# Four 256 KB transfers for each group of w_in, two groups issued one period ahead, and x's last rows sent by GpSimd's queue

## The chip, the cores and the metric

The kernel runs on one core of one Trainium2 chip. The metric is the device time of one execution in microseconds. Engine names are those of the profile: PE (TensorE), PEld (its weight loads), DVE (VectorE), ACT (ScalarE), POOL (GpSimd), SP (SyncE), which here only issues transfers; a q behind a name is the engine's queue.

## The reference, cut to what matters

Two blocks follow each other. The first is an mLSTM cell over 768 steps with 4 batches, 8 heads and a head dimension of 40; the second a feed-forward block on 3072 tokens of width 320, with 2048 inner columns.

```python
m_new = max(f + m, i);  f_stab = exp(f + m - m_new);  i_stab = exp(i - m_new)   # each step t
C = f_stab * C + i_stab * outer(v, k);   n = f_stab * n + i_stab * k
y = sigmoid(o) * (C @ q) / max(abs(n . q), 1)
...
x = y as (tokens, heads * 40)
h = x @ w_in;   g = h * cos(h);   out = g @ w_out
```

w_in (320 x 2048) and w_out (2048 x 320) come in 64-bit floats: each number is two 32-bit words, and the kernel makes 32-bit floats of them on the chip.

## The kernel before, in words

**Work and its order.** The 768 steps are six chunks of 128 (c = 0 to 5). A cell n is one chunk of one batch, n = 4c + b. The first four cells, chunk 0, are done by `first_cells` (a start-up of some 43 us). After that `both_parts(c, b)` does two things at once: the feed-forward block of chunk c, and the cell of batch b of chunk c + 1. One call of it is called a period here; it has two slots, i = 0 and i = 1, each with two of the sixteen column blocks of w_in (`f2 = 2b + i`). In a slot PE multiplies x with w_in (`Up`, L645 and L651), ACT and DVE make h cos h of it (`near` L659, `rest` L662, `sin` L667, `gate` L671), and PE multiplies an earlier slot's result with w_out (`down` L683, or in later chunks `products`, L761). The two PSUM banks of a slot are free for the next slot once both gates have run. Everything is emitted in an order written out by hand: each engine carries out its instructions in the order of the text.

**The cell.** In slot 0 come scores (L485), decay (L394, L408), values (L511 to L520) and `normalize_turned` (L529 to L540), which writes x into `xT`. `fade` (L586, four instructions on POOL) multiplies the running state by its decay; `state` (L628, four on DVE, in slot 1) adds the cell's share. Chunks 0 to 3 of the feed-forward block carry cells with fade and state; the cells of the last chunk have neither.

**x's last rows.** 256 of the 320 rows of x are in `xT`; the 64 last ones have to stand in `xL` twice, at partitions 0 and 64. For cells from the fifth on two transfers of 32 KB copy them there (L610), in `seam_out`, at the start of slot 1, from ACT's queue.

**Weights.** Chunk 0's periods also bring in the weights. w_in comes in four groups f of 512 columns. Of each, `weights_in` makes three pieces: two of 128 partitions (one for each half of 256 rows), each by four transfers of 128 KB (L139, 32 rows of 4 KB), and one for the last 64 rows by four of 64 KB (L180). w_out comes in eight pieces p by one transfer of 640 KB each (L186). Raw words land in buffers named `bits`: four buffers of pool `pb` for w_in (and, later, for the tiles `D` of `sums`), three of `pc` for w_out. A piece is converted by `take_apart` (ACT, L154 and L156), `bound` (DVE, L160 and L161) and `put_together` (DVE L167, then POOL L168). Group 1 is converted in `first_cells`, group 2 in period b = 0, group 3 in b = 1, group 4 in b = 2. Groups 3 and 4 are issued at the end of periods b = 0 and b = 1.

**Queues.** Nearly all transfers are issued by SP's queue in the text's order, so an issue that waits for a buffer holds back all behind it. In this framework the transfers of SP's and ACT's queues share eight completion semaphores in turn: a transfer is issued only when the eighth one before it has landed. Those of POOL's queue have eight of their own.

Of the kernel before, what the change touches and what calls it, by code (L numbers as in the profile page):

```python
# [11 lines left out]
FP = mybir.dt.float32  # L12
I32 = mybir.dt.int32
# [16 lines left out]
def kernel(  # L30
# [32 lines left out]

    NK = DM // 128
# [9 lines left out]
    pe = ctx.enter_context(tc.tile_pool(name="pe", bufs=3))  # L74
    po_s = ctx.enter_context(tc.tile_pool(name="po_s", bufs=4))
    p1 = ctx.enter_context(tc.tile_pool(name="p1", bufs=1))
    pb = ctx.enter_context(tc.tile_pool(name="pb", bufs=4))
    pc = ctx.enter_context(tc.tile_pool(name="pc", bufs=3))
    dram = ctx.enter_context(tc.tile_pool(name="dram", bufs=1, space=bass.MemoryType.DRAM))
    ps_a = ctx.enter_context(tc.tile_pool(name="ps_a", bufs=2, space=bass.MemoryType.PSUM))  # L80
# [50 lines left out]


    WP, WQ = 512, 2 * DM
    w_in_bits, w_out_bits = (w.bitcast(I32).rearrange("r (n two) -> r n two", two=2) for w in (moe_w_in, moe_w_out))

    def bits_in(n, src, pool, width):
        bits = pool.tile([128, width, 2], I32, name="bits", tag="bits")
        for rows, piece in src:
            nc.sync.dma_start(out=bits[rows, 0:n], in_=piece)  # L139
        return bits  # L140

    def to_float32(*made):
        for dst, bits in made:
# [27 lines left out]
    w_in_last = moe_w_in.bitcast(I32).rearrange("(h d) (a e n) -> e a h d n", d=D, e=2, n=2 * 128)[:, :, :, 32:D]  # L171

    def weights_in(f):
        for i in range(NK):
            src = [(slice(32 * a, 32 * a + 32), w_in_bits[D * (NK * a + i):D * (NK * a + i) + 32, ts(f, WP)]) for a in range(HP)]
            yield w_in_sb[:, i, ts(f, WP)], bits_in(WP, src, pb, WP)
        bits = pb.tile([128, WP, 2], I32, name="bits", tag="bits")
        for e in range(2):
            for a in range(2):
                nc.sync.dma_start(out=bits[64 * e:64 * e + 64, ts(a, 128)].rearrange("r n two -> r (n two)"), in_=w_in_last[e, 2 * f + a])  # L180
        yield w_in_l[:, ts(f, 2)].rearrange("p a n -> p (a n)"), bits


    def weights_out(p):
# [403 lines left out]
    def seam(n):  # L588
# [9 lines left out]
        if n < N - B:  # L598
# [4 lines left out]
                    nc.tensor.matmul(pu[64 * j:64 * j + D, p], kws[n][:, h, 0:D], vs(n)[:, h], start=True, stop=True)  # L603
            pus[n] = pu

    def seam_out(n):
        c, b = divmod(n, B)
        if n >= B:
            for e in range(2):
                nc.scalar.dma_start(out=xL[c][64 * e:64 * e + 64, b], in_=ys[n][0:128:2])  # L610
            return
        if b == 0:
            new_x(c)
        nc.scalar.copy(out=xT[c][:, NK * b:NK * b + NK], in_=pxs[n][:, 0:NK])
# [96 lines left out]

    def sums(c, k):

        if k % 4 == 0:
            Ds[c, k // 4] = pb.tile([128, 4, 2, C], FP, name="D", tag="bits")
        D1, D4 = (Ds[c, k // 4][:, k % 4, i] for i in range(2))
        S = Ss[c, k] = p2.tile([128, 4, C], FP, name="S", tag="S")
        G0, G1 = (gs[c, 2 * k + e].rearrange("q (p e t) -> q p e t", p=2, e=2) for e in range(2))
        tt = nc.vector.tensor_tensor
        tt(out=S[:, 2], in0=G0[:, 0, 1], in1=G1[:, 0, 1], op=OP.add)  # L720
        tt(out=S[:, 0], in0=S[:, 2], in1=G0[:, 0, 0], op=OP.subtract)
        tt(out=S[:, 3], in0=G1[:, 0, 0], in1=S[:, 0], op=OP.subtract)
        tt(out=G0[:, 0, 1], in0=G0[:, 0, 0], in1=G0[:, 0, 1], op=OP.subtract)
        tt = nc.gpsimd.tensor_tensor
        tt(out=D1, in0=G0[:, 1, 1], in1=G1[:, 1, 1], op=OP.add)  # L725
        tt(out=S[:, 1], in0=D1, in1=G0[:, 1, 0], op=OP.subtract)
        tt(out=D4, in0=G1[:, 1, 0], in1=S[:, 1], op=OP.subtract)
        tt(out=G0[:, 1, 1], in0=G0[:, 1, 0], in1=G0[:, 1, 1], op=OP.subtract)
# [2 lines left out]

    def products(c, k):

        S, D1, D4 = Ss[c, k], *(Ds[c, k // 4][:, k % 4, i] for i in range(2))
# [12 lines left out]
        banks = [id(t) for t, *_ in made]  # L747
        for j, (t, i, lhs, rhs) in enumerate(made):

            yield t[:, i], lhs, rhs, k == 0 and id(t) not in banks[:j], k == LAST and id(t) not in banks[j + 1:]  # L750

    def late_products(c):
        L = late[c] = ps_o.tile([128, 2, HALF], FP, name="late", tag="o")
        for k in range(NF // 2):
            for i, rhs in ((0, wv[:, k, 0, 1]), (1, wv[:, k, 1, 1])):
                yield L[:, i], Ds[c, k // 4][:, k % 4, i], rhs, k == 0 and i == 0, k == LAST and i == 1

    def run(made, n):
        for _ in range(n):
# [75 lines left out]
    def first_cells():  # L835
# [108 lines left out]
        turn_blocks(B)  # L944
        state(3)
        load_E(B + 2)
        decay(B)
        sigmoid(1)
        weigh_k(B)
# [16 lines left out]
    def both_parts(c, b):  # L966

        n = (c + 1) * B + b
        cell = n < N
        for i in range(2):  # L970
# [14 lines left out]
            if i == 0:  # L985
                if cell:
                    weigh(n)
                    if n + 1 < N:
                        decay_exponents(n + 1)
                    if n == B:  # L990
                        clear_low()
                for e in range(2):
                    up.sin(e)
                    up.gate(e)
                if c > 0:
                    sums(c, f2)
                if b == 0 and c == 1:
                    sigmoid(c + 1)

                if c == 0:  # L1000
                    next_out(*[pieces.pop(0) for _ in range(min(b, len(pieces), 1))])
                if cell and n + 1 < N:
                    decay(n + 1)
            else:
                if cell:
                    seam_out(n)
                if cell:
                    state(n)
                for e in range(2):
                    up.sin(e)  # L1010
                    up.gate(e)
                if c > 0:
                    sums(c, f2)
                if n == B + 1:
                    low_dimensions(n + 1)
                if c == 0:
                    next_out(*pieces)
                    pieces.clear()
                if cell and n + 1 < N:
                    if c > 0:  # L1020
                        weigh_k(n + 1)
                    odd_values(n + 1)
# [7 lines left out]
            if cell and i == 0:  # L1030
                turn_gate(n)
                values(n)
                seam(n)
                normalize_turned(n)
                fade(n)
                if c == 1 and b < 3:
                    weight_sums(b + 1)
                if n % 2 == 1 and n > B + 1 and n + 3 < N:
                    load_two(n + 3, "qk")
                if n > B + 1 and n + 3 < N:  # L1040
                    load_E(n + 3)
                if b == B - 2 and c + 2 < NC:
                    load_o(c + 2)
                if c == 0 and pieces:
                    to_float32(pieces.pop(0))
                sin_next()
            if f2 == 0 and c > 1:
                for p in range(2):
                    combine(c - 1, p)
            if i == 1:  # L1050
                if c == 0 and b + 2 < B:
                    pieces.extend(weights_in(b + 2))
                    load_two((n + 3) // 2 * 2)
# [9 lines left out]
    pieces, outs = [], []  # L1063
    with tc.manual_schedule():
        first_cells()
        for c in range(NC):
# [38 lines left out]
```

## Time and profile before

| | us |
|---|---|
| median of 3 runs (lowest, highest) | 542.03 (541.94, 544.99) |
| span of the profiled execution | 541.8 |
| PE busy | 518.0 (96%) |
| DVE busy | 420.1 (78%) |
| ACT busy | 285.1 (53%) |
| POOL busy | 227.0 (42%) |
| moved by DMA | 57.81 MB, mean 107 GB/s |

The page gives one execution, taken by the hardware profiler. Its own time is the span from the first to the last instruction; no other time of this execution is shown, and the median of the runs lies 0.2 us above it. Busy shares are means over stretches with different limits: start-up to about 43 us, the four periods of chunk 0 to about 143 us, and the rest.

### The profile page before, as it was taken

To read this page: it belongs to the slowest core of one execution; us is meant where nothing else is said; L and a number is where in the kernel's file an instruction comes from. 1 tells how busy PE (TensorE), PEld (TensorE's weight loads), DVE (VectorE), ACT (ScalarE), POOL (GpSimd) and SP (SyncE) were. 2 spreads that over 40 slices of the span, in tenths; PEclk is the share of its full clock that TensorE was granted. 3 is DMA by queue.
4 is the path that set the end of the run, shared out by engine and by line. 5 is a ranking of instruction groups with operands and counts; after the bars stand their busy time and mean duration, and the time that the engine had idled before them with its cause. 6 is when DMAs were issued, how large, how long until landed. Compare 5 with 4: busy or idle time off the path is not lost.

```text
span 541.8 us, 10496 instructions
## 1 busy us (share of the span) xinstructions
PE 518.0 (96%) x3844; PEld 349.5 (65%) x3844; DVE 420.1 (78%) x907; ACT 285.1 (53%) x546; POOL 227.0 (42%) x369
## 2 busy tenths in 40 slices
PE   7997889879999999999999999999999999999996
PEld 4874545545566666766767757757757767576755
DVE  5864978689688897898887898888898878673636
ACT  2876938496395355836436836526836522222221
POOL 7535354446376665434443533543422421221211
PEclk9968889999999999999999999999999999999999
DMA  9999759489677737519439329249320000010001
GB/s 137 209 199 222 220 151 214 131 164 246 137 124 178 104 94 168 63 68 208 46 95 189 41 82 198 44 107 178 38 93 7 2 5 6 10 41 1 0 1 48
DMA packets 99940, 57.81 MB, mean 107 GB/s; under 512 B 62305, under 2 KB 92609, under 8 KB 99889
## 3 DMA queue, kind: packets, MB, share of 16 engines
q1 hardware_dynamic: 96496, 55.64, 48.3%
q10 hardware_dynamic: 3248, 1.33, 1.2%
q8 instruction: 30, 0.49, 0.4%
q14 instruction: 22, 0.17, 0.1%
q0 software_dynamic: 144, 0.18, 0.1%
HBM read 51.71 MB, written 4.11 MB: 103 GB/s over the span
## 4 chain that ended last, share of the span: by engine, by line
PE 75%; DVE 9%; DMA 7%; POOL 2%; SPq 2%; ACT 2%; issue 2%; DVEq 0%; POOLq 0%; ACTq 0%
PE pup L651 27%; PE acc L761 23%; PE pup L645 8%; PE po L683 3%; PE ps L485 3%; PE late L761 3%; DMA E<-M_d 2%; PE vt L520 2%; DMA bits<-in_moe_w_in_dram 2%; PE vt L511 2%; DMA xL<-xT 1%; PE pu L603 1%; DVE g L671 1%; DMA vs<-in_v_dram 1%; SPq L330 1%
## 5 line engine op out<-in xcount | busy, mean ns | idle before, releaser
L651 PE MATMUL pup<-xT,w_in_sb 128*128 128x512 f32 x384 | 178.4, 607 | 5.2 <-DVE g L671 2.5
L659 ACT ACTIVATE n<-pup 128x512 int32<-128x512 f32 x96 | 53.6, 593 | 194.1 <-PE pup L645 142.6
L651 PEld LDWEIGHTS pup<-xT,w_in_sb 128*128 128x128 f32 x384 | 70.3, 192 | 93.0 <-issue 88.1
L662 DVE SCALAR_TENSOR_TENSOR n<-pup,n 128x512 f32<-128x512 f32 x96 | 62.9, 687 | 80.1 <-ACT n L659 78.7
L725 POOL TENSOR_TENSOR D<-g 128x128 f32<-128x128 f32 x40 | 19.9, 497 | 218.2 <-DVE g L671 218.2
L667 ACT ACTIVATE n<-n 128x512 f32<-128x512 f32 x96 | 57.7, 628 | 23.1 <-DVE n L662 15.4
L671 DVE SCALAR_TENSOR_TENSOR g<-pup,n 128x512 f32<-128x512 f32 x96 | 61.6, 683 | 3.9 <-ACT n L667 3.3
L761 PE MATMUL acc<-w_out_sb,g 128*128 128x160 f32 x320 | 58.6, 304 | 0.0
L761 PE MATMUL acc<-T,g 128*128 128x160 f32 x320 | 58.0, 301 | 0.1
L645 PE MATMUL pup<-xL,w_in_l 64*128 64x512 f32 x192 | 54.3, 642 | 1.3 <-POOL w_in_l L168 1.3
L761 PEld LDWEIGHTS acc<-w_out_sb,g 128*128 128x128 f32 x320 | 47.7, 190 | 5.6 <-issue 4.2
L761 PEld LDWEIGHTS acc<-T,g 128*128 128x128 f32 x320 | 48.1, 190 | 3.7 <-issue 3.0
L408 ACT ACTIVATE E<-E,tab 128x128 f32<-128x128 f32 x160 | 49.0, 389 | 0.3
L683 PE MATMUL po<-w_out_sb,g 128*128 128x320 f32 x128 | 36.4, 437 | 1.5 <-POOL w_out_sb L168 1.5
L761 PE MATMUL acc<-T,S 128*128 128x160 f32 x160 | 35.0, 300 | 0.0
L485 PEld LDWEIGHTS ps<-t,t 40*128 40x128 f32 x384 | 24.6, 188 | 12.5 <-DVE t L458 6.6
L683 PEld LDWEIGHTS po<-w_out_sb,g 128*128 128x128 f32 x128 | 23.8, 190 | 13.4 <-POOL w_out_sb L168 3.1
L645 PEld LDWEIGHTS pup<-xL,w_in_l 64*128 64x128 f32 x192 | 14.6, 186 | 25.1 <-issue 19.8
L491 DVE TENSOR_TENSOR E<-ps,E 128x512 f32<-128x512 f32 x48 | 30.6, 679 | 0.0
L761 PE MATMUL acc<-w_out_sb,S 128*128 128x160 f32 x160 | 28.8, 299 | 0.0
L958 ACT ACT_TABLE_LOAD x22 | 28.2, 1283 | 0.4
L761 PEld LDWEIGHTS acc<-T,S 128*128 128x128 f32 x160 | 26.2, 190 | 3.0 <-issue 3.0
(175 smaller groups left out, 878.8 us busy)
## 6 DMA issues: line engine op xcount, KB each, us to landing
E<-M_d SPq DMA_DIRECT2D x22, 512.0 KB
qr<-in_q_dram SPq DMA_DIRECT2D x36, 160.0 KB
kr<-in_k_dram SPq DMA_DIRECT2D x36, 160.0 KB
G<-G_d SPq DMA_DIRECT2D x20, 256.0 KB
bits<-in_moe_w_out_dram SPq DMA_DIRECT2D x8, 640.0 KB
bits<-in_moe_w_in_dram SPq DMA_DIRECT2D x32, 128.0 KB
out_dram<-o_sb SPq DMA_DIRECT2D x24, 160.0 KB
ks<-in_k_dram SPq DMA_DIRECT2D x10, 320.0 KB
```

The source lines that it names most:

```text
L408: nc.scalar.activation(out=Es[n][:, h], in_=Es[n][:, h], func=AF.Exp, scale=-1.0, bias=tab[:, c, 0, g:g + 1])
L485: nc.tensor.matmul(ps[j][:, p], kT[r, p], qT[r, p], start=True, stop=True)
L491: nc.vector.tensor_tensor(out=w, in0=pss[n][j], in1=w, op=OP.mult)
L645: nc.tensor.matmul(pu, w_in_l[r, f2], xL[c][r].rearrange("p b t -> p (b t)"), start=ahead, stop=not ahead)
L651: nc.tensor.matmul(pu.rearrange("p (b t) -> p b t", b=B), w_in_sb[:, i, ts(2 * f2 + e, 128)], xT[c][:, i:NK * B:NK], start=(i == 0 and not ...
L659: nc.scalar.activation(out=self.n[e], in_=self.pu[e], func=AF.Copy, bias=0.25)
L662: nc.vector.scalar_tensor_tensor(out=self.n[e].bitcast(FP), in0=self.pu[e], scalar=0.25, in1=self.n[e], op0=OP.add, op1=OP.subtract)
L667: nc.scalar.activation(out=r, in_=r, func=AF.Sin, scale=TWO_PI_DOWN)
L671: nc.vector.scalar_tensor_tensor(out=g, in0=self.pu[e], scalar=TWO_PI, in1=self.n[e].bitcast(FP), op0=OP.mult, op1=OP.mult)
L683: nc.tensor.matmul(po[c][b], gs[c, f][:, ts(b, C)], w_out_sb[:, f], start=(f == 0), stop=(f == NF - 1))
L761: nc.tensor.matmul(a, lhs, rhs, start=start, stop=stop)
L958: nc.scalar.activation(out=spot, in_=spot, func=AF.Sin)
```

## The change

Three things change.

- Each group of w_in is one buffer `bits` of twice the size (pool `pb` has two instead of four), filled by four transfers of 256 KB, each with 32 rows of both halves. The last 64 rows go to a tile `low` of pool `p2`, with the same four transfers of 64 KB. The tile `D` of `sums` is one for all eight k instead of two for four each.
- The transfers of group 3 are issued at the end of `first_cells`, those of group 4 in period b = 0: each one period earlier than before. The conversions keep their places.
- The two transfers of x's last rows go from ACT's queue at the start of slot 1 to POOL's queue in slot 0, right behind `normalize_turned` and ahead of `fade` (`low_out`).

```diff
-    pb = ctx.enter_context(tc.tile_pool(name="pb", bufs=4))
+    pb = ctx.enter_context(tc.tile_pool(name="pb", bufs=2))
...
+    w_in_heads = moe_w_in.bitcast(I32).rearrange("(a e d) m -> a d e m", e=NK, d=D)
...
     def weights_in(f):
-        for i in range(NK):
-            src = [(slice(32 * a, 32 * a + 32), w_in_bits[D * (NK * a + i):D * (NK * a + i) + 32, ts(f, WP)]) for a in range(HP)]
-            yield w_in_sb[:, i, ts(f, WP)], bits_in(WP, src, pb, WP)
-        bits = pb.tile([128, WP, 2], I32, name="bits", tag="bits")
+        bits = pb.tile([128, NK, WP, 2], I32, name="bits", tag="bits")
+        for a in range(HP):
+            nc.sync.dma_start(out=bits[32 * a:32 * a + 32].rearrange("r i n two -> r i (n two)"),
+                              in_=w_in_heads[a, 0:32, :, ts(f, 2 * WP)])
+        low = p2.tile([128, 2 * 128, 2], I32, name="low", tag="S")
         for e in range(2):
             for a in range(2):
-                nc.sync.dma_start(out=bits[64 * e:64 * e + 64, ts(a, 128)]..., in_=w_in_last[e, 2 * f + a])
+                nc.sync.dma_start(out=low[64 * e:64 * e + 64, ts(a, 128)]..., in_=w_in_last[e, 2 * f + a])
...
+    def low_out(n):
+        c, b = divmod(n, B)
+        for e in range(2):
+            nc.gpsimd.dma_start(out=xL[c][64 * e:64 * e + 64, b], in_=ys[n][0:128:2])
+
     def seam_out(n):
         c, b = divmod(n, B)
-        if n >= B:
-            for e in range(2):
-                nc.scalar.dma_start(out=xL[c][64 * e:64 * e + 64, b], in_=ys[n][0:128:2])
-            return
...
-        if k % 4 == 0:
-            Ds[c, k // 4] = pb.tile([128, 4, 2, C], FP, name="D", tag="bits")
+        if k == 0:
+            Ds[c] = pb.tile([128, NF // 2, 2, C], FP, name="D", tag="bits")
...
         load_E(B + 2)
+        ahead.append(weights_in(2))
...
-                if cell:
-                    seam_out(n)
...
                 normalize_turned(n)
+                low_out(n)
                 fade(n)
...
             if i == 1:
+                if c == 0 and ahead:
+                    pieces.extend(ahead.pop(0))
+                if c == 0 and b == 0:
+                    ahead.append(weights_in(3))
                 if c == 0 and b + 2 < B:
-                    pieces.extend(weights_in(b + 2))
                     load_two((n + 3) // 2 * 2)
                     load_E(n + 3)
```

More of the change, by code (lines that the diff above doesn't have):

```diff
@@ L133 @@
     WP, WQ = 512, 2 * DM
[L134 to L140, printed above, removed]
+    w_out_bits = moe_w_out.bitcast(I32).rearrange("r (n two) -> r n two", two=2)
+    w_in_heads = moe_w_in.bitcast(I32).rearrange("(a e d) m -> a d e m", e=NK, d=D)
     def to_float32(*made):
@@ L173, in weights_in @@
     def weights_in(f):
-        for i in range(NK):
-            src = [(slice(32 * a, 32 * a + 32), w_in_bits[D * (NK * a + i):D * (NK * a + i) + 32, ts(f, WP)]) for a in range(HP)]
-            yield w_in_sb[:, i, ts(f, WP)], bits_in(WP, src, pb, WP)
-        bits = pb.tile([128, WP, 2], I32, name="bits", tag="bits")
+        bits = pb.tile([128, NK, WP, 2], I32, name="bits", tag="bits")
[3 more added lines that the diff above has]
+        low = p2.tile([128, 2 * 128, 2], I32, name="low", tag="S")
         for e in range(2):
             for a in range(2):
-                nc.sync.dma_start(out=bits[64 * e:64 * e + 64, ts(a, 128)].rearrange("r n two -> r (n two)"), in_=w_in_last[e, 2 * f + a])
-        yield w_in_l[:, ts(f, 2)].rearrange("p a n -> p (a n)"), bits
+                nc.sync.dma_start(out=low[64 * e:64 * e + 64, ts(a, 128)].rearrange("r n two -> r (n two)"), in_=w_in_last[e, 2 * f + a])
+        return [(w_in_sb[:, i, ts(f, WP)], bits[:, i]) for i in range(NK)] + [(w_in_l[:, ts(f, 2)].rearrange("p a n -> p (a n)"), low)]
     def weights_out(p):
@@ L712, in sums @@
     def sums(c, k):
-        if k % 4 == 0:
-            Ds[c, k // 4] = pb.tile([128, 4, 2, C], FP, name="D", tag="bits")
-        D1, D4 = (Ds[c, k // 4][:, k % 4, i] for i in range(2))
+        if k == 0:
+            Ds[c] = pb.tile([128, NF // 2, 2, C], FP, name="D", tag="bits")
+        D1, D4 = (Ds[c][:, k, i] for i in range(2))
         S = Ss[c, k] = p2.tile([128, 4, C], FP, name="S", tag="S")
@@ L732, in products @@
     def products(c, k):
-        S, D1, D4 = Ss[c, k], *(Ds[c, k // 4][:, k % 4, i] for i in range(2))
+        S, D1, D4 = Ss[c, k], *(Ds[c][:, k, i] for i in range(2))
         G0, G1 = (gs[c, 2 * k + e].rearrange("q (p e t) -> q p e t", p=2, e=2) for e in range(2))
@@ L755, in late_products @@
             for i, rhs in ((0, wv[:, k, 0, 1]), (1, wv[:, k, 1, 1])):
-                yield L[:, i], Ds[c, k // 4][:, k % 4, i], rhs, k == 0 and i == 0, k == LAST and i == 1
+                yield L[:, i], Ds[c][:, k, i], rhs, k == 0 and i == 0, k == LAST and i == 1
     def run(made, n):
@@ L1061, in both_parts @@
                     weight_sums(0)
-    pieces, outs = [], []
+    pieces, outs, ahead = [], [], []
     with tc.manual_schedule():
```

## The prediction

> **What bounds the kernel now.** I began with the busy time of each engine by stretch. The stretches below are the end of the start-up, the four periods of part c = 0 (b = 0 to 3) and all that follows; the columns are the length, the busy time of PE, PEld, DVE, ACT and POOL (instructions in brackets), the granted clock, the DMA share and GB/s.
>
> ```profile
> 27.00:43.00 16.00, 14.49 (x132) 11.50 (x129) 10.60 (x25) 10.53 (x27) 4.77 (x5) 0.66 0.95 191
> 43.00:68.30 25.30, 21.42 (x137) 12.08 (x138) 17.95 (x39) 22.25 (x48) 11.64 (x14) 0.88 0.88 229
> 68.30:95.30 27.00, 23.33 (x146) 12.62 (x144) 21.96 (x46) 16.20 (x31) 13.84 (x13) 0.94 0.81 185
> 95.30:121.50 26.20, 21.86 (x145) 12.23 (x145) 20.31 (x44) 17.25 (x34) 12.37 (x13) 1.00 0.65 144
> 121.50:143.30 21.80, 21.57 (x145) 12.64 (x146) 18.53 (x40) 13.70 (x25) 8.86 (x10) 1.00 0.73 177
> 143.30:541.80 398.50, 392.32 (x2960) 271.26 (x2958) 312.79 (x681) 190.18 (x362) 157.71 (x276) 1.00 0.38 80
> ```
>
> From 143.3 us on PE is busy 392.3 of 398.5 us: nothing that feeds it earlier can gain much there. The period of b = 3, with no w_in left to convert, takes 21.8 us; those of b = 1 and b = 2 have the same matmuls and take 27.0 and 26.2. So the timeline of PE in these two comes next: start, duration, instruction, and in square brackets the idle time before it and who ended it.
>
> ```profile
> 72.63 3.49 PE L651 MATMUL pup<-xT,w_in_sb 128*128 128x512 f32 x4 [2.48 <-POOL w_in_sb L168]
> ...
> 95.26 3.67 PE L651 MATMUL pup<-xT,w_in_sb 128*128 128x512 f32 x8 [1.19 <-DVE g L671]
> 100.21 1.13 PE L645 MATMUL pup<-xL,w_in_l 64*128 64x512 f32 x4 [1.28 <-POOL w_in_l L168]
> ...
> 115.55 4.57 PE L683 MATMUL po<-w_out_sb,g 128*128 128x320 f32 x16 [1.47 <-POOL w_out_sb L168]
> 121.47 3.67 PE L651 MATMUL pup<-xT,w_in_sb 128*128 128x512 f32 x8 [1.34 <-DVE g L671]
> ```
>
> Converted weights and the gate come late. The timelines of ACT and DVE say why:
>
> ```profile
> 82.37 0.68 ACT L154 ACTIVATE w_in_sb<-bits 128x512 f32<-128x512 f32 x1 [2.37 <-DMA bits<-in_moe_w_in_dram]
> ...
> 108.50 0.68 ACT L154 ACTIVATE w_in_sb<-bits 128x512 f32<-128x512 f32 x1 [4.49 <-DMA bits<-in_moe_w_in_dram]
> ```
>
> ```profile
> 83.08 0.43 DVE L160 TENSOR_SCALAR w_in_sb<-w_in_sb 128x512 f32<-128x512 f32 x1 [1.37 <-ACT w_in_sb L154]
> 84.41 0.49 DVE L160 TENSOR_SCALAR w_out_sb<-w_out_sb 128x640 f32<-128x640 f32 x1 [0.43 <-ACT w_out_sb L154]
> ...
> 109.22 0.43 DVE L160 TENSOR_SCALAR w_in_sb<-w_in_sb 128x512 f32<-128x512 f32 x1 [3.48 <-ACT w_in_sb L154]
> 110.47 0.49 DVE L160 TENSOR_SCALAR w_out_sb<-w_out_sb 128x640 f32<-128x640 f32 x1 [0.36 <-ACT w_out_sb L154]
> ```
>
> ACT waits for the raw w_in of the group (third and fourth group), and DVE behind it for 1.80 and 3.84 us. The transfers were issued late because SP's queue stood at a w_out issue whose buffer was not yet free:
>
> ```profile
> 61.28 14.49 SPq L186 DMA_DIRECT2D bits<-in_moe_w_out_dram  x2
> 75.83 4.38 SPq L139 DMA_DIRECT2D bits<-in_moe_w_in_dram  x8
> ...
> 90.51 11.57 SPq L186 DMA_DIRECT2D bits<-in_moe_w_out_dram  x2
> 102.13 4.20 SPq L139 DMA_DIRECT2D bits<-in_moe_w_in_dram  x8
> ```
>
> **A: groups 3 and 4 one period ahead.** The order of the changed program puts group 3 right ahead of the issue at 61.28, and group 4 where group 3 stands now, at 75.83. Every engine's compute keeps its order. Group 3 is 1.25 MB and joins transfers that end by 70 us; behind them the DMA engines are free (third row):
>
> ```profile
> 28.00:30.00 2.00, 2.00 (x19) 1.95 (x20) 1.54 (x3) 1.96 (x5) 1.09 (x2) 1.00 0.70 168
> 30.00:32.00 2.00, 1.69 (x26) 1.45 (x24) 1.90 (x7) 1.98 (x6) 1.01 (x2) 1.00 0.56 161
> ...
> 70.00:72.00 2.00, 0.15 (x1) 0.00 (x0) 1.99 (x4) 0.00 (x0) 0.76 (x1) 1.00 0.05 16
> ```
>
> At the 185 to 229 GB/s of the periods' rows it takes 5.5 to 6.8 us, so it is in place by about 76 us, and ACT needs it at 80.00 (82.37 - 2.37). Group 4 lands some 20 us ahead of its use at 104. The w_out piece pushed back by eight issues is converted only from 96 us on. Both DMA waits of ACT go, and with them DVE's.
>
> What PE gets of it: in b = 1 DVE and POOL run 1.80 us earlier up to the gate at 94.42, so PE's 1.19 goes whole. The 1.28 in front of L645 shrinks: its weights come 1.80 earlier, PE 1.19, so 1.28 - 0.61 = 0.67 stays. In b = 2 the chain is 1.80 + 3.84 = 5.64 earlier and PE 1.80: there are 3.84 us to cover the waits of 1.47 and 1.34 (2.81), so both go. A = 1.19 + 0.61 + 1.47 + 1.34 = 4.61. The 2.48 at 72.63 stays: it belongs to group 2, whose data was there, and is DVE's order of work. Bounds: 0 if the data comes no earlier, 5.28 if the 0.67 goes too.
>
> **B: four transfers of 256 KB.** By the semaphores of the built program a transfer of SP or ACT waits for the eighth one before it. With 128 KB and 64 KB pieces eight in flight are few bytes, and at 28 to 32 us the DMA engines were busy only 0.70 and 0.56 of the time, which leaves 0.60 + 0.88 = 1.48 us unused, in a stretch (27 to 43 us, first row of all) where their share is 0.95. Four issues fewer, twice as large, let SP run ahead there. What follows in the queue ends in x's gates o, for which ACT waits:
>
> ```profile
> 50.23 1.28 ACT L321 ACT_TABLE_LOAD   x1 [2.51 <-DMA o<-in_o_gate_dram]
> ```
>
> In the rest of this period ACT is busy 22.25 of 25.30 us and sets its pace, so what o gains, PE gains. Bounds 0 and 1.48 (of the 2.51); I take 1.2, near the upper one because that share is so high: what is issued earlier there also lands earlier. Against it: the first half of a group now waits for all four transfers, not for the first four of eight. That is at most half the group later, but the group as a whole is not, and ACT comes to it after both halves have landed.
>
> **C: x's last rows by GpSimd.** Two issues per cell leave ACT's queue and stand on POOL between the weights' or sums' work and the fade of the state; they wait for xT (L540), and behind them wait the four fade instructions, for these DVE's state update (L628), for it the gate (L671), and for its first half PE's next L651. Twenty cells have the pair. What POOL pays for one pair, here the two of G, and when such transfers land:
>
> ```profile
> 21.01 1.10 POOL L264 DMA_DIRECT2D G_d<-kr  x2
> ```
>
> ```profile
> M_d<-kr POOLq DMA_DIRECT2D x1, 80.0 KB, 4.3
> G_d<-kr POOLq DMA_DIRECT2D x2, 40.0 KB, 2.8
> ```
>
> Call a pair's price x; the row says 1.10 us (80 runs of 512 B each; xL has 64). The tightest part is c = 1:
>
> ```profile
> 174.56 1.38 POOL L586 TENSOR_TENSOR st<-st,tab 40x128 f32<-40x128 f32 x4
> ...
> 177.22 1.01 DVE L540 TENSOR_TENSOR xT<-yt,db 128x384 f32<-128x384 f32 x1
> ...
> 180.39 0.86 DVE L628 TENSOR_TENSOR st<-st,pu 40x128 f32<-40x128 f32 x4
> 181.28 1.29 DVE L671 SCALAR_TENSOR_TENSOR g<-pup,n 128x512 f32<-128x512 f32 x2
> ...
> 182.21 3.60 PE L651 MATMUL pup<-xT,w_in_sb 128*128 128x512 f32 x8
> ```
>
> The fade ends at 178.23 + x + 1.38; the last of the four updates begins at 180.39 + 0.65 = 181.04, and PE has 0.28 more (first gate done at 181.93, PE at 182.21). So PE waits from x = 1.71 on. In c = 2 and 3 there are 5.03 us from L540's end to PE against 3.98 here, so from x = 2.76:
>
> ```profile
> 255.06 0.56 DVE L540 TENSOR_TENSOR xT<-yt,db 128x384 f32<-128x384 f32 x1
> ...
> 260.65 3.60 PE L651 MATMUL pup<-xT,w_in_sb 128*128 128x512 f32 x8
> ```
>
> In c = 0, b = 1, the same sum with these rows:
>
> ```profile
> 89.40 1.98 POOL L586 TENSOR_TENSOR st<-st,tab 40x128 f32<-40x128 f32 x4
> 90.12 0.56 DVE L540 TENSOR_TENSOR xT<-yt,db 128x384 f32<-128x384 f32 x1
> 93.53 0.87 DVE L628 TENSOR_TENSOR st<-st,pu 40x128 f32<-40x128 f32 x4
> 94.42 1.29 DVE L671 SCALAR_TENSOR_TENSOR g<-pup,n 128x512 f32<-128x512 f32 x2
> ```
>
> 94.18 - 90.68 - 1.98 = 1.52, and once A has run PE comes 0.80 after the first gate: from x = 2.32. With x = 1.10 nothing waits: the price is 0, hidden by the 0.6 to 1.2 us that are left. The landing (2.8 to 4.3 us) is far ahead of the next use, two matmul slots later. I add 0.2 for extra contention of POOL and DVE; lower bound 0, since ACT's later queue is off the path. ACT gains the time of two issues, which PE does not see.
>
> The Trainium skill (page "SBUF — State Buffer", section "SBUF: two separate sides") speaks against C: while VectorE is in a 2-port mode GpSimd cannot write the descriptors of its own transfers, and one that takes about 620 ns alone takes about 3100 ns beside a VectorE copy. No row here shows it; by its figure x would be about 6.2 in c = 0, where L160 follows L540 at once, which is an estimate of +11.6 us over three cells and 548 us in all.
>
> **Sum.** The profiled execution's span is 541.8; the median of the runs, 542.03, lies 0.2 above it. 541.8 - 4.61 - 1.2 + 0.2 = 536.2, and 536.4 as a median.
>
> **Rivals.** (1) DVE is the bound once the waits are gone. For it: it is busy 21.96 and 20.31 us in the two periods, and beside POOL its instructions can stretch, as the row of L167 shows (minimum, median, maximum in ns):
>
> ```profile
> L167 DVE SCALAR_TENSOR_TENSOR w_out_sb<-bits,w_out_sb x8: 816/822/1900, 58.3 to 143.4; 128x640 int32<-128x640 int32 x8
> ```
>
> One such stretch (1.08) in each period and B at 0: 541.8 - 4.61 + 2.16 + 0.2 + 0.2 = 539.8. Against it: b = 2 has 1.03 us in hand. (2) Slower: POOL is held until its transfer lands. Then x is 2.8 to 4.3; at 3.55, three cells of c = 0 lose 1.23, four of c = 1 lose 1.84, eight of c = 2 and 3 lose 0.79: 17.4 us, or 553.6. It decides from about x = 2.8, where the losses (6.1) eat the gain. Against it: the pair of G took 1.10 with landings of 2.8. (3) The early issue brings nothing, as the DMA engines are full then: 542. Against it: the share of 0.05 at 70 us. (4) More: o gains all 2.51, and the four L651 at 72.63, 0.87 us each against 0.46 in the row at 95.26, run at full clock (1.66 less): 541.8 - 4.61 - 2.51 - 1.66 + 0.2 = 533.2. Against it: the 2.48 ahead of them stays.
>
> **How the numbers follow.** Forecast 59%, with its own range 535.0 to 537.8; (1) 17%, (4) 12%, (2) 8%, (3) 4%. One per cent of 542.03 is 5.4 us, so 536.6 is the limit, about what a measurement of this kernel can tell from no change; two thirds of the forecast's chance lie below it, as I left out small waits of PE that A also shortens. Faster: 39 + 12 = 51%. Within: 20 + 17 + 4 = 41%. Slower: 8%. The range, 533.6 to 540.2, leaves out (2), (3) and the far side of (4).
>
> **What would show it.** Right: no DMA wait of ACT at L154 in b = 1 and b = 2, periods of about 22 us, o's wait near 1.3 us, a pair of xL issues at 1.1 us on POOL, no wait of L628 for the fade. Wrong: PE waiting for L671 behind L586 in c = 1 (C's step), or b = 1 and b = 2 as long as before with the data there (A's step).

## The result, and the profile after

| | before | after |
|---|---|---|
| median of the runs, us | 541.99 | 539.40 (537.49 to 540.78) |
| span of the profiled execution, us | 541.8 | 538.5 |
| ratio of the times, first comparison | 1 | 0.993, 95% interval 0.9907 to 0.9953 |
| ratio, second comparison (`changed_again` below) | 1 | 0.991, 95% interval 0.9882 to 0.9939 |

The change brings 0.7 to 0.9% by the two ratios (the two medians of the first row alone give 0.5%): inside the range of the prediction, 3 us short of its 536.4, and on the side "within 1%" that it held for the less likely. Single executions of the kernel before lie at 541.6 to 545.7 us, so the ratios, and not two medians, are what to compare. The profiled execution of `ab_low_by_act` below ran at a mean clock of 0.649 (757 us) and a second one took 1824 us, so both are left out of its ratio and its steps are read from `ab_again`, the same kernel.

The busy time by stretch, after, columns as in the prediction (its last column pairs are granted clock, DMA share, GB/s):

```profile
27.00:43.00 16.00, 15.90 (x168) 14.06 (x167) 8.82 (x23) 13.38 (x33) 6.56 (x6) 0.82 1.08 189
43.00:68.30 25.30, 24.55 (x163) 12.96 (x163) 19.59 (x45) 21.51 (x47) 12.65 (x16) 0.83 1.02 250
68.30:95.30 27.00, 23.19 (x146) 13.14 (x146) 23.46 (x49) 18.47 (x37) 14.96 (x16) 0.94 0.88 173
95.30:121.50 26.20, 25.35 (x157) 13.98 (x157) 24.19 (x51) 17.73 (x33) 16.11 (x18) 1.00 0.97 201
121.50:143.30 21.80, 21.80 (x152) 13.14 (x149) 16.52 (x34) 12.84 (x24) 10.74 (x14) 1.00 1.08 200
143.30:538.50 395.20, 388.80 (x2947) 269.46 (x2944) 311.75 (x677) 191.28 (x362) 171.18 (x305) 1.00 0.35 75
```

The stretches are those of the prediction, so after the change the same stretch holds more of the work: that of b = 2 has 157 of PE's instructions instead of 145, and PE is busy for 25.35 instead of 21.86 of its 26.20 us. PE's timeline shows which waits are left (line numbers are 3 or 4 lower than before: L648 was L651, L642 was L645):

```profile
57.06 0.42 PE L507 MATMUL vt<-E,vs 128*32 128x128 f32 x8 [0.43 <-issue]
69.31 1.10 PE L648 MATMUL pup<-xT,w_in_sb 128*128 128x512 f32 x2 [0.93 <-DVE g L668]
74.14 2.56 PE L648 MATMUL pup<-xT,w_in_sb 128*128 128x512 f32 x4 [2.88 <-POOL w_in_sb L163]
99.42 1.13 PE L642 MATMUL pup<-xL,w_in_l 64*128 64x512 f32 x4 [0.64 <-POOL w_in_l L163]
...
138.42 3.60 PE L648 MATMUL pup<-xT,w_in_sb 128*128 128x512 f32 x8
```

The waits of 1.19, 1.47 and 1.34 us are gone, the 1.28 is 0.64, the 2.48 has stayed (2.88), and one of 0.93 is new. ACT's conversions of groups 3 and 4 begin with no wait, since the transfers were issued 18 us (58.25 against 75.83) and 25 us (77.36 against 102.13) earlier:

```profile
81.29 0.66 ACT L149 ACTIVATE w_in_sb<-bits 128x512 f32<-128x512 f32 x1
...
103.13 0.67 ACT L149 ACTIVATE w_in_sb<-bits 128x512 f32<-128x512 f32 x1
```

```profile
58.25 2.23 SPq L171 DMA_DIRECT2D bits<-in_moe_w_in_dram  x4
...
77.36 1.87 SPq L171 DMA_DIRECT2D bits<-in_moe_w_in_dram  x4
```

For all that follows, three marks on PE's timeline divide an execution: the first values of the period b = 0 (57.06 above), the first `Up` of c = 1 (138.42 above), and the end. Before, the first two stand here:

```profile
55.63 0.46 PE L511 MATMUL vt<-E,vs 128*32 128x128 f32 x8 [3.88 <-issue]
...
143.09 3.60 PE L651 MATMUL pup<-xT,w_in_sb 128*128 128x512 f32 x8
```

So the start-up went from 55.63 to 57.06 (+1.43), chunk 0 from 87.46 to 81.36 (-6.10), and what follows from 541.8 - 143.09 = 398.7 to 538.5 - 138.42 = 400.1 (+1.4): the gain is in chunk 0, and two losses take nearly half of it back. By the first values of each period, b = 0 takes 27.09 us (27.01 before), b = 1 22.21 (24.54), b = 2 21.02 (24.87), and from there to the second mark it is 11.04 in both. So the gain of chunk 0 is in b = 1 (2.33) and b = 2 (3.85), at full clock in both kernels. These two periods, before and then after (columns as above):

```profile
82.64:107.18 24.54, 21.82 (x145) 12.24 (x144) 20.17 (x43) 17.02 (x33) 12.66 (x13) 1.00 0.77 167
107.18:132.05 24.87, 21.82 (x145) 12.24 (x144) 21.48 (x46) 18.60 (x34) 12.14 (x12) 1.00 0.96 213
```

```profile
84.15:106.36 22.21, 21.36 (x145) 12.41 (x144) 20.09 (x45) 17.69 (x34) 13.28 (x15) 1.00 0.93 187
106.36:127.38 21.02, 21.02 (x145) 12.51 (x144) 19.15 (x42) 15.20 (x28) 13.06 (x14) 1.00 1.12 205
```

The +1.43 of this execution goes with the clock. Two slices of four microseconds of each kernel, before and then after (columns as above):

```profile
12.00:16.00 4.00, 4.00 (x38) 3.10 (x36) 3.92 (x7) 2.80 (x4) 0.00 (x0) 1.00 0.97 173
32.00:36.00 4.00, 3.89 (x30) 3.02 (x30) 2.29 (x5) 2.62 (x10) 1.29 (x1) 0.50 0.98 225
```

```profile
12.00:16.00 4.00, 4.00 (x31) 3.24 (x30) 3.93 (x8) 3.08 (x3) 0.00 (x0) 0.75 0.91 178
16.00:20.00 4.00, 4.00 (x18) 3.42 (x17) 1.60 (x3) 2.65 (x4) 3.94 (x6) 0.50 1.10 282
```

After, the clock falls to 0.50 at 14 us, where PE sets the pace (18 matmuls in 4 us); before, it fell at 32 us, where PE then waited anyway (the 3.88). When it falls is a matter of the execution: `ac_128kb`, `ac_pair_behind_sums` and `ac_idle_pair` below issue the same work in the start-up and have it at 14, 20 and 32 us. In the five profiles with 14 us, the table load at which ACT else waits for the o gates comes at 51.6 us with no wait, and the start-up ends at 56.97 to 57.06 us; `c_alone`, with neither early groups nor large transfers, is one of them. In the eight others ACT waits there, and the edit counts: the start-up ends at 53.99 to 55.63 us with 128 KB (four profiles) and at 55.12 to 57.15 with 256 KB (four). So the changed kernel's start-up is late by the clock here, and it is late with a later clock too (57.15 in `low_after_sums`). Why the clock falls when it does, no run here tells.

### The profile page after: what moved, and what is told of

Same layout as the page of the kernel before. It is cut to its first block, busy times and chain, and to the rows that moved or that the text cites. A ratio compares the mean times of both kernels' runs of the same rounds, so it can differ in the third digit from the quotient of the medians.

```text
span 538.5 us, 10486 instructions
## 1 busy us (share of the span) xinstructions
PE 522.8 (97%) x3844; PEld 354.4 (66%) x3844; DVE 419.5 (78%) x907; ACT 287.1 (53%) x546; POOL 247.8 (46%) x409
## 4 chain that ended last, share of the span: by engine, by line
PE 76%; DMA 10%; DVE 8%; SPq 3%; POOL 2%; ACT 1%; issue 1%; DVEq 0%; POOLq 0%
PE pup L648 27%; PE acc L758 22%; PE pup L642 8%; PE po L680 5%; PE ps L481 3%; DMA bits<-in_moe_w_in_dram 3%; PE late L758 3%; PE vt L516 2%; PE vt L507 2%; DVE t L454 1%; DMA low<-in_moe_w_in_dram 1%; PE pu L599 1%; DMA G<-G_d 1%; DMA bits<-in_moe_w_out_dram 1%; DVE g L668 1%; DMA E<-M_d 1%
## 5 line engine op out<-in xcount | busy, mean ns | idle before, releaser
L648 PE MATMUL pup<-xT,w_in_sb 128*128 128x512 f32 x384 | 178.3, 607 | 4.0 <-POOL w_in_sb L163 2.9
L648 PEld LDWEIGHTS pup<-xT,w_in_sb 128*128 128x128 f32 x384 | 70.7, 192 | 91.3 <-issue 84.4
L664 ACT ACTIVATE n<-n 128x512 f32<-128x512 f32 x96 | 59.3, 630 | 16.0 <-DVE n L659 16.0
L642 PE MATMUL pup<-xL,w_in_l 64*128 64x512 f32 x192 | 55.7, 651 | 0.6 <-POOL w_in_l L163 0.6
L605 POOL DMA_DIRECT2D xL<-xT x40 | 22.4, 561 | 72.6 <-DVE xT L536 68.6
L481 PEld LDWEIGHTS ps<-t,t 40*128 40x128 f32 x384 | 26.4, 198 | 13.5 <-DVE t L454 7.2
L642 PEld LDWEIGHTS pup<-xL,w_in_l 64*128 64x128 f32 x192 | 15.0, 187 | 24.5 <-issue 21.3
L481 PE MATMUL ps<-t,t 40*128 40x128 f32 x384 | 28.7, 289 | 1.1 <-DVE t L454 0.8
```

The costliest lines, as they stand in the source:

```text
L481: nc.tensor.matmul(ps[j][:, p], kT[r, p], qT[r, p], start=True, stop=True)
L605: nc.gpsimd.dma_start(out=xL[c][64 * e:64 * e + 64, b], in_=ys[n][0:128:2])
L642: nc.tensor.matmul(pu, w_in_l[r, f2], xL[c][r].rearrange("p b t -> p (b t)"), start=ahead, stop=not ahead)
L648: nc.tensor.matmul(pu.rearrange("p (b t) -> p b t", b=B), w_in_sb[:, i, ts(2 * f2 + e, 128)], xT[c][:, i:NK * B:NK], start=(i == 0 and not ...
L664: nc.scalar.activation(out=r, in_=r, func=AF.Sin, scale=TWO_PI_DOWN)
```

## The experiments

Three parts make eight combinations. A is the early issue, B the 256 KB transfers (without B a group still has its one buffer, but eight transfers of 128 KB), C x's last rows (xL) by GpSimd. Ratios are to the kernel before in the same comparison; the lengths are those between the marks, in one profiled execution.

| kernel | parts | ratio (95%) | start-up | chunk 0 | from c = 1 on |
|---|---|---|---|---|---|
| before | none | 1 | 55.63 | 87.5 | 398.7 |
| `a_alone` | A | 1.0064 (1.0040 to 1.0088) | 54.55 | 92.5 | 398.7 |
| `b_alone` | B | 1.0115 (1.0084 to 1.0146) | 55.12 | 92.9 | 398.7 |
| `c_alone` | C | 1.0023 (1.0005 to 1.0040) | 57.00 | 87.0 | 399.8 |
| `ab_again` | A, B | 1.0022 (1.0006 to 1.0037) | 56.99 | 87.6 | 398.7 |
| `ac_128kb` | A, C | 0.9880 (0.9855 to 0.9905) | 56.97 | 79.9 | 399.8 |
| `bc_old_places` | B, C | 1.0166 (1.0143 to 1.0189) | 56.21 | 93.5 | 399.7 |
| after | A, B, C | 0.9930 (0.9907 to 0.9953) | 57.06 | 81.4 | 400.1 |
| `changed_again` | A, B, C | 0.9910 (0.9882 to 0.9939) | 56.99 | 79.8 | 399.8 |
| `low_after_sums` | A, B, C late | 0.9905 (0.9878 to 0.9932) | 57.15 | 80.4 | 398.7 |
| `ac_pair_behind_sums` | A, C late | 0.9874 (0.9844 to 0.9905) | 54.57 | 82.7 | 398.7 |
| `ac_idle_pair` | A, C, and a pair on ACT | 1.0067 (1.0041 to 1.0093) | 53.99 | 91.0 | 399.7 |
| `a_pair_behind_loads` | A, xL by ACT in later turns | 0.9866 (0.9835 to 0.9898) | 57.06 | 81.5 | 398.7 |

No part alone makes the kernel faster; A and C together do.

### xL back on ScalarE's queue: `ab_low_by_act`, and again as `ab_again`

```diff
-                low_out(n)
...
+                if cell:
+                    seam_out(n)      # n >= B: nc.scalar.dma_start(out=xL[c]..., in_=ys[n][0:128:2]), twice
```

> The changed kernel with one part undone: the copy of x's last rows (xL) goes by ScalarE's queue at its old place; early groups and 256 KB transfers stay. Theory 1: the GpSimd pair costs 1.35 us, all of it in chunk 1, because it waits for xT (3.5 us) at the head of GpSimd and holds the fade and the column sums of w_out behind it, which then run beside VectorE's own sums (0.76 and 0.92 us instead of 0.29 and 0.43). Then this kernel takes about 538.0 us, and the stretch from chunk 1's first up-projection to chunk 2's start is 1.35 us shorter than in the changed kernel. Rival: the pair is free, as the prediction had it, and the 1.35 us are the scatter of a single execution: 539.4 us.

Measured: 1.0022 (0.9998 to 1.0046). Both theories were wrong: taking C back doesn't gain 1.4 us, it loses the whole gain.

> The early groups and the 256 KB transfers with xL by ScalarE's queue, once more, because the first profiled execution ran at a mean clock of 0.65 and its steps can't be laid beside the others'. Open: why this kernel isn't faster than before (1.002) when the changed kernel (0.993) differs only in who sends xL. Theory 1: in chunk 0, with w_in's groups queued earlier, ScalarE's pair of issues or the wait for xT ahead of it sits in front of the conversion of w_in and w_out, and PE waits for that (3 to 5 us in sum over b=0 to b=2); the chunks from 1 on take 398.7 us as in the kernel before. Theory 2: the start-up is late here (the low dimensions and the o gate land later), and xL has no part in it: then PE's first up-projection or its wait for vt is 3 us or more later than in the kernel before, and the periods b=1 and b=2 are as short as in the changed kernel.

Measured: 1.0022 (1.0006 to 1.0037), chunk 0 at 87.6 us, and 398.7 from c = 1 on, as theory 1 had it. SP's timeline and its waits between 56 and 92 us (waited for, total us, times, longest) say why:

```profile
61.52 12.47 SPq L171 DMA_DIRECT2D bits<-in_moe_w_in_dram  x4
...
91.84 0.93 SPq L338 DMA_DIRECT2D qr<-in_q_dram  x2
```

```profile
SPq L171 <- DMA xL<-xT: 8.3, 1, 8.3
SPq L338 <- DMA xL<-xT: 4.2, 1, 4.2
```

```profile
101.78 2.08 PE L646 MATMUL pup<-xL,w_in_l 64*128 64x512 f32 x4 [4.08 <-POOL w_in_l L163]
```

SP waits for the landing of xL, which it has no use for: the transfers of SP and ACT take turns on eight completion semaphores, and the transfer eight turns back is ACT's pair. q's blocks (qr) go out at 91.84 us, in the changed kernel at 82.97, ACT waits for them, and the last rows of group 3, converted behind them on ACT, make PE wait 4.08 us. Theory 1 expected something on ACT's own queue; it is SP that stands still. Theory 2 (a late start-up) has 1.4 us of it (56.99 against 55.63), here with ACT waiting 4.54 us for o.

### The early issue alone: `a_alone`

```diff
-        for a in range(HP):
-            nc.sync.dma_start(out=bits[32 * a:32 * a + 32]..., in_=w_in_heads[a, 0:32, :, ts(f, 2 * WP)])
+        for i in range(NK):
+            for a in range(HP):
+                nc.sync.dma_start(out=bits[32 * a:32 * a + 32, i]..., in_=w_in_heads[a, 0:32, i, ts(f, 2 * WP)])
```

and xL by ScalarE as in the kernel above.

> Only the early issue of groups 3 and 4 (with the one buffer), in eight 128 KB transfers a group as before; xL by ScalarE. The prediction's term: -4.6, 537.4 us. Theory 1: the trace shows -5.9 for this part between b=1 and b=3, so 536 to 537.5, and within 0.7 us of the kernel that has the early issue and the 256 KB transfers. Rival: the 256 KB transfers cost the start-up 1.35 us, and this kernel is that much faster than that one; or they bring 1.2 us, and it is that much slower.

Measured: 1.0064, slower than before, against 537.4 expected. Timelines of SP, ACT and PE, and SP's wait between 70 and 100 us:

```profile
74.82 17.76 SPq L172 DMA_DIRECT2D bits<-in_moe_w_in_dram  x8
...
95.24 1.22 SPq L339 DMA_DIRECT2D qr<-in_q_dram  x2
```

```profile
SPq L172 <- DMA xL<-xT: 10.5, 2, 10.1
```

```profile
97.89 0.40 ACT L447 COPY qr<-qr 32x256 f32<-32x256 f32 x1 [5.55 <-DMA qr<-in_q_dram]
```

```profile
105.44 2.08 PE L647 MATMUL pup<-xL,w_in_l 64*128 64x512 f32 x4 [7.85 <-POOL w_in_l L163]
```

Group 4 is queued behind b = 1's pair in the turn of the semaphores: its seventh and eighth transfers take the pair's turns, and the pair waits for b = 1's xT, near 90 us. SP holds there for 10.1 us, with qr behind it, and PE pays 7.85 us. With eight transfers a group more turns are spent than with four, so the early issue alone fares worse than A with B.

### The large transfers alone: `b_alone`

```diff
-        ahead.append(weights_in(2))
...
-                if c == 0 and ahead:
-                    pieces.extend(ahead.pop(0))
-                if c == 0 and b == 0:
-                    ahead.append(weights_in(3))
                 if c == 0 and b + 2 < B:
+                    pieces.extend(weights_in(b + 2))
```

> Only the 256 KB transfers (with their one buffer): every group is issued at its old place, xL by ScalarE. The prediction's term for this part is -1.2 us: 540.8. Theory 1 (the start-up of the changed kernel was late because the throttle came at 13 us instead of 32, which the transfers don't set): 541 to 542, with PE's waits for w_in's conversion in b=1 and b=2 as in the kernel before. Rival: the large transfers hold up the start-up's small loads and cost 1.35 us: 543.4.

Measured: 1.0115, some 6 us slower: neither theory. The timelines of SP, ACT and PE:

```profile
75.36 1.87 SPq L171 DMA_DIRECT2D bits<-in_moe_w_in_dram  x4
```

```profile
84.74 0.67 ACT L149 ACTIVATE w_in_sb<-bits 128x512 f32<-128x512 f32 x1 [5.24 <-DMA qr<-in_q_dram]
...
113.54 0.67 ACT L149 ACTIVATE w_in_sb<-bits 128x512 f32<-128x512 f32 x1 [7.22 <-DMA bits<-in_moe_w_in_dram]
```

```profile
91.80 4.57 PE L684 MATMUL po<-w_out_sb,g 128*128 128x320 f32 x16 [2.75 <-POOL w_out_sb L163]
...
120.58 6.26 PE L684 MATMUL po<-w_out_sb,g 128*128 128x320 f32 x16 [4.21 <-POOL w_out_sb L163]
```

From the first issue to ACT's start there are 84.74 - 75.36 = 9.4 us, where the kernel before had 82.37 - 75.83 = 6.5: each large transfer carries rows of both halves, so the first conversion waits for the whole group. (The releaser named at 84.74 is the transfer that came last by the profile; ACT's instruction reads only the group.) ACT's waits are 5.24 and 7.22 instead of 2.37 and 4.49, and the w_out pieces converted behind come 2.75 and 4.21 us late for PE. The start-up is no later (55.12): the rival is wrong too.

### Two parts without the third: `ac_128kb`, `bc_old_places`, `c_alone`

The edits are those shown above, on the changed kernel (for `c_alone`, `low_out` put into the kernel before).

> The changed kernel with eight 128 KB transfers a group instead of four of 256 KB. With xL by ScalarE the early issue in 128 KB transfers held SyncE for 20 us (74.8 to 95.2 us), qr landed after that, and ScalarE, waiting for it, held the last rows of group 3: PE stood still for 7.85 us. Theory 1: the number of transfers ahead of qr on SyncE's queue sets this, and xL's queue doesn't: the stall is here too, some 3.5 us over before (545 to 547). Rival: xL's place makes the stall: no stall over 2 us, 538 to 540.

Measured: 0.9880, 79.9 us for chunk 0, and no wait of PE over 1 us but the one for group 2 (2.88). The rival of this expectation is right: xL's place makes the stall, and the number of transfers ahead of qr doesn't.

> The changed kernel with groups 3 and 4 issued at their old places. With xL by ScalarE the 256 KB transfers at the old places took 1.0115 of before: ScalarE waited 7.2 and 5.2 us for the group's bits, because both halves of a group land together, and held the conversion of w_out behind it (PE waits of 2.75 and 4.21 us). Theory 1: this has nothing to do with xL, so 1.012 to 1.016 (549 to 551 us) here too. Rival: GpSimd's xL brings 4 to 5 us in chunk 0 whatever the groups do: 544 to 546.

Measured: 1.0166. B costs at the old places whichever queue sends xL.

> The kernel before with xL sent by GpSimd at the changed kernel's place, nothing else. If the part costs what the changed kernel's chunk 1 shows and brings nothing elsewhere: +1.36 us (1.0025), chunks 1 to 3 taking 400.1 us instead of 398.7. If taking xL off ScalarE is what brings chunk 0 its gain: 3 to 5 us faster before chunk 1, 539 to 541 in all.

Measured: 1.0023, 399.8 us from c = 1 on, and 87.0 us in chunk 0 against 87.5: C brings nothing where nothing is issued early, and has its cost in c = 1.

### Is it the turns? `ac_idle_pair` and `a_pair_behind_loads`

The first adds to A and C, in chunk 0, a pair on ScalarE's queue at its old place into a tile that nobody reads; the second sends xL by ScalarE, but emits the pair of b = 1 and b = 2 behind the loads.

```diff
+                if cell and c == 0:
+                    for e in range(2):
+                        nc.scalar.dma_start(out=idle[64 * e:64 * e + 64], in_=ys[n][0:128:2])
```

```diff
-                if cell:
+                if cell and not (c == 0 and b in (1, 2)):
                     seam_out(n)
...
                     load_E(n + 3)
+                if cell and c == 0 and b in (1, 2):
+                    seam_out(n)
                 if cell and n + 1 < N:
                     turn_blocks(n + 1)
```

> The changed kernel in 128 KB transfers (0.988 of before), and besides, in chunk 0, ScalarE copies the same rows of xT at its old place into a tile that nobody reads. Theory 1 (the queue): all transfers that SyncE and ScalarE issue take turns on eight semaphores, and each waits until the one eight before it has landed; so SyncE, in the middle of group 4, waits for ScalarE's pair of the same period, which waits for xT. Then the idle pair alone brings back SyncE's 18 us in group 4's issue, qr's late landing and the PE stall of 7 to 8 us: 546 to 549 us. Rival (what was gained by moving xL to GpSimd is ScalarE's 0.6 us before its sine activations, or xL's own landing): no stall over 2 us, 537 to 539.

Measured: 1.0067, 547.2 us. One pair of 32 KB copies that no one reads brings the whole loss back. SP's timeline, its waits and PE's timeline:

```profile
74.28 14.80 SPq L172 DMA_DIRECT2D bits<-in_moe_w_in_dram  x8
```

```profile
SPq L172 <- DMA idle<-xT: 14.5, 2, 7.4
```

```profile
102.11 2.08 PE L643 MATMUL pup<-xL,w_in_l 64*128 64x512 f32 x4 [8.05 <-POOL w_in_l L163]
```

> Early groups in 128 KB transfers, xL by ScalarE everywhere (1.0064 of before in that form), but in the periods b=1 and b=2 of chunk 0 its pair stands behind w_in's group and the loads of q, k and v in the program's order, so that it takes later turns of the eight semaphores. Theory 1: SyncE isn't held in group 4, the PE stall of 7.85 us goes, and chunks 1 to 3 take 398.7 us since GpSimd has no pair ahead of its fade: 535 to 537 us. Rival (ScalarE mustn't send xL at all): the stall stays at 4 us or more, 541 to 548.

Measured: 0.9866, 536.65 us. With later turns ScalarE may send xL: group 4 goes out in 4.32 us, qr at 84.64, and PE's wait is 0.79:

```profile
77.32 4.32 SPq L172 DMA_DIRECT2D bits<-in_moe_w_in_dram  x8
...
84.64 0.94 SPq L339 DMA_DIRECT2D qr<-in_q_dram  x2
```

```profile
99.53 1.13 PE L647 MATMUL pup<-xL,w_in_l 64*128 64x512 f32 x4 [0.79 <-POOL w_in_l L163]
```

The two together show the cause: who sends xL doesn't matter, whose turn of the shared semaphores it takes does.

### What C costs in c = 1: `low_after_sums` and `ac_pair_behind_sums`

```diff
-                low_out(n)
                 fade(n)
                 if c == 1 and b < 3:
                     weight_sums(b + 1)
+                low_out(n)
```

In the changed kernel GpSimd's pair waits for xT with the fade and the column sums of w_out behind it. POOL's and DVE's timelines there:

```profile
154.59 1.12 POOL L605 DMA_DIRECT2D xL<-xT  x2 [4.01 <-issue]
155.73 1.39 POOL L582 TENSOR_TENSOR st<-st,tab 40x128 f32<-40x128 f32 x4
...
160.04 0.87 POOL L707 TENSOR_TENSOR T<-w_out_sb,T 128x320 f32<-128x320 f32 x1
```

```profile
159.35 0.76 DVE L717 TENSOR_TENSOR S<-g 128x128 f32<-128x128 f32 x1
160.14 0.92 DVE L718 TENSOR_TENSOR S<-S,g 128x128 f32<-128x128 f32 x1
```

> The changed kernel with the GpSimd pair for xL moved behind the fade and the column sums, still on GpSimd. Theory 1 (the loss of chunk 1 is in what the pair holds up while it waits for xT): the fade and the sums are back at their old times, the pair finds xT ready, 538.0 us. Rival (it is the 1.1 us of the pair's own issue on GpSimd, wherever it stands): 539.4 us. If a pair this late makes xL late for the next up-projection, the PE waits at its first low matmul for xL and the time is over 539.4.

Measured: 0.9905 (0.9878 to 0.9932), and 398.7 us from c = 1 on, exactly the length before. The pair still takes POOL 1.11 us, and DVE's sums are back at their old length:

```profile
155.06 1.11 POOL L605 DMA_DIRECT2D xL<-xT  x2
```

```profile
158.18 0.29 DVE L717 TENSOR_TENSOR S<-g 128x128 f32<-128x128 f32 x1
158.50 0.43 DVE L718 TENSOR_TENSOR S<-S,g 128x128 f32<-128x128 f32 x1
```

> The changed kernel in 128 KB transfers with GpSimd's pair behind the fade and the column sums. In 256 KB transfers that order gave back 1.36 us of chunk 1. Theory 1: here too, 535.5 to 536.3 us, and chunks 1 to 3 take 398.7 us instead of the 399.8 of the kernel with 128 KB transfers and the pair ahead. Rival: the order saves nothing where the transfers are small: 537.

Measured: 0.9874 (0.9844 to 0.9905), 537.83 us where 542 to 545.7 were measured for before, and 398.7 us again from c = 1 on. In the six profiles with the pair ahead of the fade the length is 399.7 to 400.1, in the seven others (the kernel before among them) 398.7. In the times themselves the 1.0 to 1.4 us, 0.2%, are too small to tell: the intervals of 0.9880 and 0.9874 overlap.

### The changed kernel once more: `changed_again`

> The changed kernel once more, beside the kernels above on one chip: 0.993 of before, 539.4 us. Theory 1: the 256 KB transfers by themselves cost 1 to 2 us against 128 KB (0.988), because both halves of a group land together, so that the first conversion waits for the whole group. Rival: the difference of the two ratios is that of two chips, and both kernels take the same time beside each other.

Measured: 0.9910. Its marks (56.99, 136.82, 536.6) are within 0.02 us those of `ac_128kb` (56.97, 136.82, 536.6), whose clock fell at the same points: with the groups issued early and the clock down at 14 us, the size of the transfers changes nothing that these two profiles show. The times leave open whether 256 KB still costs a little: 0.9910 against 0.9880, and 0.9905 against 0.9874 with the pair behind the sums, point that way, but the intervals overlap. The two profiles of the changed kernel differ by 1.9 us in span, of which 1.5 lie in chunk 0: its b = 0 takes 25.42 us here, at a mean clock of 1.00, and 27.09 in the first profile, at 0.94. Its b = 1 and b = 2, at full clock in both, take 22.35 and 21.02 us (22.21 and 21.02 there).

## Why the prediction was right or wrong

**The bound (PE waits for w_in in b = 1 and b = 2)** was read rightly. Of SP's two long holds the first (61.28, 14.49 us) was for the w_out buffer, as the prediction says; of the second (90.51, 11.57 us) 5.6 us were a wait for xL. The kernels that issue the groups early with SP free have b = 1 and b = 2 without PE's waits, but for the 0.6 to 0.8 in front of xL's matmuls.

**A (-4.61): right in its mechanism, too small, and wrong in a condition that wasn't named.** With C, the waits came out as the step had them: 1.19, 1.47 and 1.34 gone, 0.64 left where 0.67 was expected, the one of group 2 left (2.88 for 2.48). b = 1 and b = 2 gained 2.33 and 3.85 us, 6.18 together, where the step had 1.80 and 2.81: it counted the listed waits alone, while PE's unused time fell by 1.87 and 3.05 us and its busy time, at the same clock, by 0.46 and 0.80. In b = 0, which the step left alone, the 0.93 at 69.31 us is new. But alone A costs 0.64%. The step followed the queue's order and the DMA engines' load; it didn't ask on whose landing each early issue would have to wait. The rule of the eight semaphores stood in the prediction's part B, and SP's waits of the kernel before held the row that should have led there (5.6 us for a transfer that SP has no use for):

```profile
SPq L186 <- DMA xL<-xT: 5.6, 1, 5.6
```

**B (-1.2): wrong.** The step was that fewer issues let SP run ahead in the start-up, so that the o gate lands earlier. SP runs ahead less: the loads of q and k stand eight turns behind w_in's transfers, which are now twice as large, and in all six profiles with 256 KB SP waits 2.1 to 2.8 us for those to land (between 20 and 46 us); in the seven with 128 KB it waits for w_in 0.2 us at most. After:

```profile
SPq L338 <- DMA bits<-in_moe_w_in_dram: 2.8, 4, 0.9
```

The first issue of o goes out at 42.33 to 44.25 us with 256 KB, and at 40.85 to 41.45 in six of the seven with 128 KB (42.55 before). ACT's table load behind the wait for o begins at 49.72 with B alone and at 50.23 before, which is no more than the scatter; with the groups issued early and a clock that falls late it begins at 51.58 and 51.74 with 256 KB, and at 48.59 to 49.17 with 128 KB. Its "against it" (the first half of a group waits for all four transfers) was called harmless because ACT comes late enough; that holds with A only. At the old places it costs 1.1 to 1.4% (1.0115, and 1.0166 against 1.0023). The Trainium skill (page "DMA: Bandwidth & Descriptors", section "Rules for kernel authors") advises to coalesce many small transfers into one large one, and puts the overhead mostly under 64 KB; between 128 and 256 KB these runs show no gain from it, and a loss where a reader could have begun with half of the data.

**C (+0.2): mis-sized in one place and missed in another.** The pair's price x was right (1.11 to 1.19 us on POOL against 1.10), and rightly free from c = 2 on. In c = 1 it costs 1.0 to 1.4 us: the sum asked when DVE's state update would wait for the fade, and it never does, but the column sums of w_out, which stand behind the fade, moved some 5 us (the last one from 0.8 to 6.0 us behind the end of xT's writing in b = 0: the pair's wait of 3.5 to 4.0 and its 1.1) and met DVE's own sums (0.29 and 0.43 us became 0.76 and 0.92). Behind those stand the transposes that the scores read, and in `changed_again` PE waits 0.21 and 0.19 us for them; how the rest of the loss reaches PE, no row here shows. And the condition that C gives A, its true worth, wasn't seen: A with C is 0.9880, A without it 1.0064.

**Sum.** With A at 6.18, C at 1.4 and, in B's place, the 1.43 that this execution's start-up lost, the same sum gives 541.8 - 6.18 + 1.4 + 1.43 = 538.5, the measured span. The forecast of 536.2 is no further off because its errors oppose each other: A was 1.6 too small, B and C each 1.2 too favourable. That is luck.

**The rivals.** (1) DVE as the bound, 539.8, is near in its number, yet not by its mechanism: what stretched on DVE were the sums in c = 1, not the conversions (the longest takes 1.90 us in both kernels). (2) GpSimd held until landing: wrong; xL's issues (minimum, median, maximum in ns) and landings, after:

```profile
L605 POOL DMA_DIRECT2D xL<-xT x40: 542/564/634, 64.8 to 453.7; - x40
...
DMA to landing us min/median/max: 1.7/3.9/9.1
```

POOL goes on after 0.56 us an issue, long before the data lands. The rule of the Trainium skill that spoke for a dearer pair ("SBUF — State Buffer", section "SBUF: two separate sides", some 3.1 us for one such transfer beside a VectorE copy) did not show in POOL's own time, on which the prediction had put it: the longest of the 40 issues took 0.63 us. The landings, of which that section speaks, do vary, from 1.7 to 9.1 us; whether VectorE is the reason no run here separates, and no wait of PE for xL followed. (3) Nothing from the early issue: wrong here; A alone brings nothing either, but by SP's hold, not by full DMA engines. (4) More: o gained nothing; but that the four L651 behind the 2.48 ran at a reduced clock was right, as at a full one (`changed_again`) they take 1.98 us together, not 3.49:

```profile
74.03 1.98 PE L648 MATMUL pup<-xT,w_in_sb 128*128 128x512 f32 x4 [2.88 <-POOL w_in_sb L163]
```

## What to carry to other kernels

Where queues share a ring of semaphores, an early transfer waits for the landing of the one that held its turn before, whichever queue sent it: before you hoist a load, list the turns between it and its use, and move late, data-dependent transfers to another ring or to later turns. Large transfers are free only where all of their data is there before the first reader comes and no later load waits for their turns. An instruction put ahead of others on an in-order engine is priced by its wait and by what then runs beside something else, not by its own duration.

## What the runs showed of the hardware that was not expected

PE's clock fell to half during the start-up, at 32 us in the profile before and at 14 us in the one after, with PE busy 4.00 of 4.00 us (as the profile models it) when it fell in the latter; the slice at half clock holds 18 matmuls where the same four microseconds before held 42. Over the thirteen profiles it fell at 14 us (five), 20 (three) or 32 (five), also among kernels with the same start-up. The matmuls of the start-up are in the same order in both; the slice before:

```profile
16.00:20.00 4.00, 4.00 (x42) 3.77 (x40) 2.75 (x8) 3.61 (x6) 3.46 (x6) 1.00 1.08 267
```

Beside GpSimd's sums of 128 x 320, VectorE's sums of 128 x 128 took 0.76 and 0.92 us instead of 0.29 and 0.43.
